# A plan of rounds for every batch: projection pieces, value runs and the mixer's steps placed anew

## The chip, the core and the metric

The kernel runs on one NeuronCore of a Trainium2 chip. The metric is the device time of one execution in microseconds (us). The kernel before was timed three times: 812.35 us is the median, 811.07 and 813.69 us are the ends.

A NeuronCore has five engines that take their instructions in order, each from its own queue: TensorE (PE, matrix products and transposes), VectorE (DVE), ScalarE (ACT), GpSimd (POOL), and SyncE (SP), which issues most DMAs. They wait for one another through semaphores.

## The reference

Three blocks follow each other, on 4 batches of 768 tokens with 512 channels.

```python
# 1. chunked local attention, 8 heads of 64: chunks of 32 queries see 16 keys to the left, 8 to the right, 8 memory keys
a = softmax(scale * q_c @ concat(mem_k, k_ctx).T);  out[chunk] = a @ concat(mem_v, v_ctx)
# 2. four experts of causal attention (width 64), each token keeps its best two
logits = x @ w_gate                       # top 2 of 4, softmax over them
for e in range(4):
    q, k, v = x @ wq[e], x @ wk[e], x @ wv[e]
    ye = softmax(causal(scale * q @ k.T)) @ v @ wo[e]
    out += gate[e] * ye
# 3. mixer: a rank-32 product along the sequence, then a two-layer network of 2048 hidden channels
u = x + (x.T @ U @ V).T
out = u + relu(u @ w_ch1) @ w_ch2
```

## The kernel before

The first part of the program, up to some 415 us of the span, does blocks 1 and 2 and the sequence mixing of block 3; the rest does the two-layer network. Only the first part is touched here.

Each batch goes through 12 *rounds*. A round belongs to a pair of experts and a tile of 128 query tokens: `ROUNDS` lists tiles 0 to 2 of pair 0, tiles 0 to 2 of pair 1, then tiles 3 to 5 of both. The function `rnd` writes the instructions of one round:

- a *unit* of local attention (two heads, half the sequence, of the next batch, or of batch 0 in the first rounds): scores `s` (L534), softmax in `a`, transposes `tp` (L562) that are copied to `at`;
- the round's expert scores `sc` (L673 and L675), softmax in `ac` (DVE L694, ACT L696, POOL L731);
- the transposes `tpc` (L751) of the round before, copied to `ath` (L754) by ACT and DVE in turn;
- up to three *pieces* of work taken from a list: a projection of queries and keys (`pqk`, L593) or of values (`pv`, L633);
- in some rounds a *run*: the products that use only a part of the array's columns, one after the other, into `t` and `t2` (L829): local values (`t<-at`), expert values (`t<-ath`), and the mixer's first product (`t<-y`).

The run is written with a higher priority, and its first product waits for all copies that any product of the run reads (`READY` in `rnd`); the products behind it follow in order.

Which round has a run is said by `SESSIONS`, how many pieces a round takes by `FILL` (batch 0: `FILL0`), which round starts a unit by `S_AT`. A run takes the expert values of rounds that were transposed before the last one; for a pair (batch, round) in `FRESH` it takes the last one's too.

The mixer has, for each pair of a batch, four steps: `mix_turn` transposes the result `yT` (`pyt`, L779) and copies it to `y`; `mix_down` multiplies `y` with U as a part of a run; `mix_keep` makes `qm` of it on ACT and DVE; `mix_up` multiplies `qm` with V (`pz`, L809), adds and stores it. Their rounds stand in the loop as numbers that hold for all batches: turn of pair 1 in round 2 of the next batch, its down in round 3, its up in round 7 (last batch: 4); turn of pair 0 in round 10, its down in round 11, its up in round 0 of the next batch.

In the last batch, pieces of the network's first product (`ph`, L366; `po`, L383) and of the product of weights (`w1p`, L313) fill the rounds.

The Tile framework's scheduler then orders each engine's instructions, so rounds overlap in the built program. PSUM tiles rotate between two buffers: `sc`, `tpc`, `pyt` and the wide `pz` share one pair, `s` and `tp` another. A tile's first write waits until the readers of the tile two before it are done.

Of the kernel before, what the change touches and what calls it, by code (L numbers as in the profile page):

```python
# [29 lines left out]
NT = S // 128  # L30
# [8 lines left out]
NIDLE = 4  # L39
WLOAD = {1: ((0,), ()), 2: ((1,), ()), 3: ((2, 3), ()), 5: ((), (0, 1))}  # L40
WSPLIT = {2: ((0,), ()), 3: ((1, 2), ()), 4: ((3,), ()), 5: ((), (0, 1))}
FILL = (1, 1, 2, 1, 1, 1, 1, 1, 1, 1, 1, 2)
S_AT0 = (2, 3, 4, 5, 6, 7, 9, 10)
FILL0 = (0, 0, 0, 3, 2, 2, 0, 1, 2, 1, 2, 1)
S_AT = (0, 1, 3, 4, 5, 6, 8, 9)
NAC = 7
AHEAD = 400
NLIN = 2
# [3 lines left out]
NLT = 5  # L52
NLA = 1
NAT = 8
SESSIONS = {0: (0, 2, 4, 6, 8, 9, 11), 1: (1, 3, 5, 7, 9, 11), 2: (1, 3, 5, 7, 9, 11), 3: (1, 3, 5, 7, 9, 11)}
FRESH = ((0, 9), (1, 9), (2, 9), (3, 9), (3, 11))
NXP = 8
FS = 1
HG = 1
# [45 lines left out]
def tile_chunk_attention__moe_attention__mixer(  # L105
# [309 lines left out]
    with ExitStack() as p1:  # L415
# [349 lines left out]
        def keep(b, pr, i, pav):  # L765
            if i == 0:
                pool, kw_ = (cw, dict(bufs=2)) if b % 2 or (b, pr) == (B - 2, 1) else (dp0, dict(tag=f"wp_{'hl'[pr]}0", bufs=1))
                yT[b, pr] = pool.tile([128, S], F32, name="yT", **kw_)
            nc.scalar.copy(yT[b, pr][:, i * 128:(i + 1) * 128], pav)

        ys, qms, ys_ins = {}, {}, {}

        def mix_turn(b, pr):
            y = ys[b, pr] = cw.tile([128, NT, 128], F32, name="y", tag="ac", bufs=NAC)
            p = ps.tile([128, 1024], F32, name="pyt", **TC)
            for t in range(NT):
                tr = nc.tensor.transpose(p[:, t * 128:(t + 1) * 128], yT[b, pr][:, t * 128:(t + 1) * 128], ident_s)  # L779
            hold['p4'] = tr.ins  # L780
            ys_ins[b, pr] = [nc.scalar.copy(y[:, :4], p[:, :512].rearrange("p (t f) -> p t f", f=128)).ins,
                             nc.vector.tensor_copy(y[:, 4:], p[:, 512:768].rearrange("p (t f) -> p t f", f=128)).ins]
# [50 lines left out]
        def rnd(new=None, old=None, s_unit=None, o_unit=None, fill1=(), fill2=(), down=None, then=None, late=(), locs=()):  # L833
            if s_unit:
                local_load(s_unit)
                if then:
                    load_weights(*then)
                local_scores(s_unit, 0)
            turned = []

            def between():
                if o_unit:
                    local_turn(o_unit, 0)
                turned.append(1)
            if new:
                scores(*new, between)
            if not turned:
                between()
            if s_unit:
                local_scores(s_unit, 1)  # L850
            if o_unit:
                local_turn(o_unit, 1)
            for f in fill1:
                f()
            if old:
                turn_scores(*old)
            for f in fill2:
                f()
            if not (locs or late or down):
                return  # L860
            free = [ps.tile([128, 512], F32, name="t", **TE)]
            if len(locs) == 2 or locs and len(late) + bool(down) > 1:
                free.append(ps.tile([128, 512], F32, name="t2", **TQ))
            pos = [x[:, :HALF] for x in free[:len(locs)]]
            places = [x[:, o:o + 128] for n, x in enumerate(free) for o in ((HALF,) if n < len(locs) else (HALF, 256, 128, 0))]
            with tc.high_priority(AHEAD):
                session.clear()
                behind = [x for v in late for x in turned_ins.pop(v)] + [x for u in locs for x in half[u]["ins"]]
                if down:
                    behind += ys_ins.pop(down[:2])  # L870
                kept = [(v, places.pop(0)) for v in late]
                for n in range(max(len(locs), 1)):
                    if locs:
                        local_values(locs[n], pos[n])
                    for v, p in kept[n:n + 1] if n + 1 < len(locs) else kept[n:]:
                        values(*v, p)
                if down:
                    pq = places.pop(0)
                    mix_down(*down, pq)
                for x in behind:  # L880
                    tc.add_manual_dep(session[0], x.name, READY, reason="start of a run on parts of the array")
                for x, y in zip(session, session[1:]):
                    tc.add_manual_dep(y, x.name, QUEUE, reason="run on parts of the array")
            for v, p in kept:
                keep(*v, p)
            for u, p in zip(locs, pos, strict=True):
                local_split(u, p)
            if down:
                mix_keep(*down, pq)
# [38 lines left out]
        def batch_half(b, hf):  # L928
            return [(b, hp, hf) for hp in range(HP)]
# [3 lines left out]
        for _ in range(NWARM):  # L933
            p = ps.tile([128, 512], F32, name="pwarm", **TL)
# [19 lines left out]
                nc.vector.memset(row_s[:, :S - 128], 0.0)  # L954
                nc.vector.tensor_copy(row_s[:, S - 128:], tri_s)
        load_mixer()
        old, mixed, turned, locs = None, {}, [], []
        for b in range(B):
            last = b == B - 1
            s_at = {} if last else dict(zip(S_AT0 if b == 0 else S_AT, batch_half(b + 1, 0) + batch_half(b + 1, 1)))  # L960
            before = None
            if b == 0:
                s_at.update(zip(range(8), units[PRO:]))
                before = units[PRO - 1]
            work = pieces(b, 1) + ([] if last else pieces(b + 1, 0))
            for r, (pr, i) in enumerate(ROUNDS):
                n = (FILL0 if b == 0 else FILL)[r] if work else 0
                ending[0] = last and r >= 10
                f1, f2, work = work[:n][:1], work[:n][1:], work[n:]
                if b and r == 2:  # L970
                    f2 = f2 + [lambda: mix_turn(b - 1, 1)]
                if b and r == (4 if last else 7):
                    f1 = [lambda: mix_up(b - 1, 1)] + f1
                if r == 10:
                    f2 = f2 + [lambda: mix_turn(b, 0)]
                if b and r == 0 and not mixed.get(b - 1):
                    f1 = [lambda: mix_up(b - 1, 0)] + f1
                down = (b, 0) if r == 11 else (b - 1, 1) if b and r == 3 else None
                o_unit = s_at.get(r - 1) if r else before
                locs += [o_unit] if o_unit else []  # L980
                now, wait = turned, [old] if old else []
# [2 lines left out]
                if r in SESSIONS[b]:  # L984
                    rnd((b, pr, i), old, s_at.get(r), o_unit, f1, f2, down, late=now, locs=locs)
                    turned, locs = wait, []
                else:
                    rnd((b, pr, i), old, s_at.get(r), o_unit, f1, f2)
                    turned = turned + [old] if old else turned
                old = (b, pr, i)  # L990
# [35 lines left out]
    with ExitStack() as p2:  # L1026
# [45 lines left out]
        late = list(range(NEC, NCH))  # L1072
# [80 lines left out]
        for k, (c, f) in enumerate(steps):  # L1153
# [36 lines left out]
            if store and not todo:  # L1190
                (c_, pt_), = store
                store = []
                if not nx:
                    with tc.issue_after(ended[0]):
                        pr = [residual(c_, m, TLAST[m]) for m in range(KT)]
                else:
                    pr = None
# [79 lines left out]
```

## Time and profile before

| | |
|---|---|
| median of three runs | 812.35 us (811.07 to 813.69) |
| the profiled execution | 814.0 us, of which the span from the first to the last instruction is 811.9 us |
| PE busy | 784.9 us, 97% of the span |
| DVE, ACT, POOL busy | 620.5, 497.2, 159.4 us |
| share of the chain that ended last | PE 70%, DVE 16%, ACT 6%, DMA 5% |

A row of the timeline names the start, the time that the row's instructions took together, the engine, the source line, the operation, what it writes and reads, and how often. In brackets stands how long the engine sat idle before the row, and whose instruction released it. A matmul's recorded time is longer than its step to the next one, since matmuls overlap. Products of fp32 operands (`s`, `t`) have two records each.

### The profile page before, as it was taken

What the parts mean: (1) busy time and instruction counts of PE and PEld (TensorE: products, weight loads), DVE (VectorE), ACT (ScalarE), POOL (GpSimd) and SP (SyncE); (2) the same over time, 40 slices, a digit from 0 to 9 for tenths busy, and PEclk for the clock granted to TensorE, in tenths of its full rate; (3) what the DMA queues carried; (4) which work ended last, traced back from release to release, by engine and by line L of the source; (5) the groups of instructions that cost most, each with busy time, mean ns of one, the idle gap of its engine ahead of it and who ended that gap; (6) DMA issues with size and microseconds to landing.
All of it is one profiled execution on the core that took longest, in us unless ns stands there. A gap on an engine that the chain in (4) does not pass through costs nothing.

```text
span 811.9 us, 17863 instructions
## 1 busy us (share of the span) xinstructions
PE 784.9 (97%) x6382; PEld 710.2 (87%) x6382; DVE 620.5 (76%) x2029; ACT 497.2 (61%) x1448; POOL 159.4 (20%) x244
## 2 busy tenths in 40 slices
PE   7989999999999999998999999999999999999997
PEld 5779998989999897887888888999999999999996
DVE  6687878687778769996468799989587595875956
ACT  6787767677668756665445567665455564555642
POOL 4554434444343513313000000000000000000000
PEclk9999999999999999999999999999999999999999
DMA  9443353333333105153037635103003030030211
GB/s 287 123 149 95 92 144 110 93 91 111 92 96 100 43 9 219 53 175 130 15 115 236 199 101 181 53 1 131 1 4 128 1 114 16 2 131 1 78 53 52
DMA packets 36792, 77.67 MB, mean 96 GB/s; under 512 B 4192, under 2 KB 12896, under 8 KB 35936
## 3 DMA queue, kind: packets, MB, share of 16 engines
q1 hardware_dynamic: 36416, 76.21, 29.1%
q8 instruction: 50, 0.82, 0.4%
q14 instruction: 38, 0.31, 0.1%
q10 hardware_dynamic: 288, 0.32, 0.1%
HBM read 60.79 MB, written 15.73 MB: 94 GB/s over the span
## 4 chain that ended last, share of the span: by engine, by line
PE 70%; DVE 16%; ACT 6%; DMA 5%; issue 3%; POOL 0%; DVEq 0%; ACTq 0%; POOLq 0%; SPq 0%
PE acc L1150 25%; PE ph L366 14%; PE t L829 6%; PE pqk L593 5%; PE pv L633 3%; PE s L534 3%; PE po L383 3%; PE tpc L751 3%; DMA raw<-in_w 2%; PE sc L673 2%; PE sc L675 2%; PE tp L562 2%; ACT a L541 2%; DVE d_t L144 1%; DMA part<-o 1%
## 5 line engine op out<-in xcount | busy, mean ns | idle before, releaser
L1150 PE MATMUL acc<-xhi,sw 128*128 128x256 f32 x1008 | 187.9, 282 | 0.1
L1150 PEld LDWEIGHTS acc<-xhi,sw 128*128 128x128 f32 x1008 | 159.3, 189 | 4.8 <-ACT xhi L1068 0.3
L1150 PE MATMUL acc<-xlo,sw 128*128 128x256 f32 x504 | 139.1, 282 | 0.2 <-DVE xlo L1069 0.2
L1065 DVE TENSOR_TENSOR sx<-t 128x256 f32<-128x256 f32 x180 | 67.9, 423 | 66.8 <-ACT t L1058 66.7
L1058 ACT ACTIVATE t<-ph 128x512 f32<-128x512 f32 x72 | 43.0, 598 | 99.4 <-PE ph L366 99.3
L1150 PEld LDWEIGHTS acc<-xlo,sw 128*128 128x128 f32 x504 | 95.5, 190 | 2.4 <-DVE xlo L1069 0.4
L731 POOL TENSOR_SCALAR ac<-ac,su,g 128x128 f32<-128x128 f32 (+5 forms) x92 | 69.0, 758 | 104.8 <-DVE su L729 27.5
L1068 ACT CAST xhi<-sx 128x256 fp32r<-128x256 f32 x205 | 74.8, 406 | 22.0 <-DVE sx L1065 19.0
L541 ACT ACTIVATE a<-a,nm 128x96 f32<-128x96 f32 x192 | 69.9, 366 | 20.1 <-DVE nm L538 19.7
L1069 DVE TENSOR_TENSOR xlo<-sx,xhi 128x256 fp32r<-128x256 f32 x205 | 77.0, 424 | 3.0 <-ACT xhi L1068 2.2
L366 PE MATMUL ph<-zh,wp_l 128*128 128x512 f32 x192 | 61.4, 398 | 0.3 <-DVE hl L376 0.3
L366 PE MATMUL ph<-zh,wp_h 128*128 128x512 f32 x192 | 60.9, 394 | 0.0
L751 PE MATMUL tpc<-ident_s,ac 128*128 128x128 f32 x336 | 53.1, 277 | 6.3 <-POOL ac L731 2.6
L696 ACT ACTIVATE ac<-ac,nmc 128x128 f32<-128x128 f32 (+5 forms) x72 | 47.8, 665 | 17.9 <-DVE nmc L694 17.3
L546 POOL TENSOR_TENSOR a<-a,rs 128x288 f32<-128x288 f32 x64 | 43.2, 678 | 77.3 <-DVE rs L545 35.8
L534 PE MATMUL s<-k_t,q_t 128*128 128x96 f32 (+1 forms) x480 | 52.3, 269 | 5.1 <-DMA k_t<-in_kw 1.5
L366 PE MATMUL ph<-zl,wp_h 128*128 128x512 f32 x176 | 55.6, 394 | 0.0
L534 PEld LDWEIGHTS s<-k_t,q_t 128*128 128x128 f32 (+1 forms) x480 | 46.5, 172 | 10.0 <-issue 5.3
L694 DVE CUSTOM_DVE_ANT_0 ac<-sc,row_s 128x128 f32<-128x128 f32 (+5 forms) x72 | 43.3, 618 | 11.0 <-PE sc L675 10.5
L538 DVE CUSTOM_DVE_ANT_0 a<-s,band_s 128x96 f32<-128x96 f32 x192 | 39.8, 250 | 14.5 <-PE s L534 13.8
L751 PEld LDWEIGHTS tpc<-ident_s,ac 128*128 128x128 f32 x336 | 38.5, 141 | 13.6 <-POOL ac L731 5.8
L673 PE MATMUL sc<-kl,qs 128*128 128x384 f32 (+2 forms) x144 | 48.2, 340 | 1.3 <-DVE ath L754 0.6
(209 smaller groups left out, 1952.5 us busy)
## 6 DMA issues: line engine op xcount, KB each, us to landing
raw<-in_w SPq DMA_DIRECT2D x42, 256.0 KB, 3.6
v_t<-in_vw SPq DMA_DIRECT2D x32, 288.0 KB, 4.1
q_t<-in_qT SPq DMA_DIRECT2D x24, 384.0 KB, 3.2
k_t<-in_kw SPq DMA_DIRECT2D x31, 220.0 KB, 3.5
part<-o SPq DMA_DIRECT2D x24, 256.0 KB, 2.9
pt<-part SPq DMA_DIRECT2D x6, 1024.0 KB, 4.8
out<-pt SPq DMA_DIRECT2D x24, 256.0 KB, 2.3
raw<-in_w SPq DMA_DIRECT2D x11, 512.0 KB, 3.8
```

The costliest lines, as they stand in the source:

```text
L366: nc.tensor.matmul(p, w[f // 4][:, pr, fs], z[:, pr], start=(n == 0), stop=(n == 5))
L534: last = nc.tensor.matmul(s[own, j, :], w["q"][own, qd * 3 + j], k_g[own], start=True, stop=True).ins
L541: nc.scalar.activation(a[:, j, :], a[:, j, :], AF.Exp, bias=nm[:, j:j + 1], scale=-1.0, accum_out=ss[:, j:j + 1])
L673: nc.tensor.matmul(s[:, o:o + w], q, kl[b, e, hf][:, :w], start=True, stop=False)
L696: nc.scalar.activation(a, a, AF.Exp, bias=nm[:, h:h + 1], scale=-1.0, accum_out=su[:, h:h + 1])
L731: (nc.vector if ending[0] else nc.gpsimd).tensor_scalar(aa[h][:, :n], aa[h][:, :n], su[:, h:h + 1], gates[b, i // 3][:, i % 3, 2 * pr + h: ...
L751: hold['t', 6 * (i // 3) + 3 * pr + i % 3] = nc.tensor.transpose(tp[h][:, j * 128:(j + 1) * 128], aa[h][:, j * 128:(j + 1) * 128], ident_s ...
L829: session.append(nc.tensor.matmul(*a, **kw).ins)
L1065: nc.vector.tensor_tensor(x, t[:, p[0], p[1]], t[:, q[0], q[1]], op=op)
L1068: nc.scalar.copy(hi, x)
L1069: nc.vector.tensor_sub(lo, x, f32(hi))
L1150: ended[0] = nc.tensor.matmul(acc[n][:, m], w[:, ms], x, start=(f == FA and u == 0 and m == 0), stop=(f == NF - 2 and u == 2 and m == 1)).ins
```

## The change

The tables get one entry per batch, and the rounds of the mixer's steps become tables too. `SESSIONS` has other rounds in batches 0, 1 and 3; `FRESH` has 12 pairs where it had 5. Nothing is computed differently: each engine has the same instructions with the same operands' shapes, in another order. The rename from `kept` to `keeps` makes room for a counter that is checked while the program is built.

```diff
-FILL = (1, 1, 2, 1, 1, 1, 1, 1, 1, 1, 1, 2)
...
-FILL0 = (0, 0, 0, 3, 2, 2, 0, 1, 2, 1, 2, 1)
...
+FILL = ((0, 0, 0, 3, 1, 2, 0, 2, 0, 3, 1, 2),
+        (1, 1, 3, 1, 1, 0, 0, 2, 1, 1, 1, 2),
...
-SESSIONS = {0: (0, 2, 4, 6, 8, 9, 11), 1: (1, 3, 5, 7, 9, 11), 2: (1, 3, 5, 7, 9, 11), 3: (1, 3, 5, 7, 9, 11)}
-FRESH = ((0, 9), (1, 9), (2, 9), (3, 9), (3, 11))
+SESSIONS = {0: (1, 2, 4, 5, 6, 7, 9, 10, 11), 1: (0, 1, 3, 4, 5, 7, 9, 11), 2: (1, 3, 5, 7, 9, 11), 3: (1, 3, 5, 10, 11)}
+FRESH = ((0, 0), (0, 9), (0, 10), (0, 11), (1, 3), (1, 9), (2, 9), (3, 3), (3, 5), (3, 7), (3, 9), (3, 11),)
+TURN1, DOWN1, UP1 = (5, 2, 2, 2), (2, 4, 3, 3), (3, 9, 9, 5)
+TURN0, DOWN0, UP0 = (10, 10, 10, 11), (11, 11, 11, 11), (4, 2, 3, 0)
...
-                n = (FILL0 if b == 0 else FILL)[r] if work else 0
+                n = FILL[b][r]
...
-                if b and r == 2:
+                if b and r == TURN1[b]:
                     f2 = f2 + [lambda: mix_turn(b - 1, 1)]
-                if b and r == (4 if last else 7):
+                if b and r == UP1[b]:
                     f1 = [lambda: mix_up(b - 1, 1)] + f1
-                if r == 10:
+                if r == TURN0[b]:
                     f2 = f2 + [lambda: mix_turn(b, 0)]
-                if b and r == 0 and not mixed.get(b - 1):
+                if b and r == UP0[b]:
                     f1 = [lambda: mix_up(b - 1, 0)] + f1
-                down = (b, 0) if r == 11 else (b - 1, 1) if b and r == 3 else None
+                down = (b, 0) if r == DOWN0[b] else (b - 1, 1) if b and r == DOWN1[b] else None
```

In the built order the network part behind 415 us is the same on PE. In the first part PE has 44 runs of part-array products before, and 40 now. Three places follow; the line numbers of the kernel now are 3 to 6 higher.

PE from the end of batch 0 into batch 1, before: the run that ends with the mixer's first product, and what follows up to `pz`.

```order
L829 MATMUL t_2228<-at,v_t 64x64 x12
L829 MATMUL t_2228<-y,u_s 32x128 x6
...
L751 MATMUL tpc<-ident_s,ac 128x128 x12
L534 MATMUL s<-k_t,q_t 128x96 x3
L562 MATMUL tp<-ident_s,a 96x128 x3
L673 MATMUL sc<-kl,qs 128x256
L675 MATMUL sc<-kd,qs 128x256
L673 MATMUL sc<-kl,qs 128x256
L675 MATMUL sc<-kd,qs 128x256
L751 MATMUL tpc<-ident_s,ac 128x128
L809 MATMUL pz<-v_st,qm 128x384 x2
```

The same place now.

```order
L835 MATMUL t_2254<-y,u_s 32x128 x6
L565 MATMUL tp<-ident_s,a 96x128 x3
L596 MATMUL pqk<-xl,wqk_h 128x384 x4
L596 MATMUL pqk<-xh,wqk_h 128x384 x4
L596 MATMUL pqk<-xh,wqk_l 128x384 x4
...
L596 MATMUL pqk<-xl,wqk_h 128x384 x4
L596 MATMUL pqk<-xh,wqk_h 128x384 x4
L596 MATMUL pqk<-xh,wqk_l 128x384 x4
...
L835 MATMUL t<-at,v_t 64x64 x12
L835 MATMUL t<-ath,vt 64x128 x12
...
L815 MATMUL pz<-v_st,qm 128x384
```

Two projection pieces and a run, which stood behind `pz`, now stand between the mixer's first product and `pz`.

PE in round 3 of batch 3, before: the run that ends with the mixer's first product for the pair 1 of batch 2.

```order
L633 MATMUL pv<-wvg_l,xh 128x260
L673 MATMUL sc<-kl,qs 128x128
L675 MATMUL sc<-kd,qs 128x128
L673 MATMUL sc<-kl,qs 128x128
L675 MATMUL sc<-kd,qs 128x128
...
L829 MATMUL t<-ath,vt 64x128 x6
L829 MATMUL t<-y,u_s 32x128 x6
L751 MATMUL tpc<-ident_s,ac 128x128 x3
L366 MATMUL ph<-zh,wp_l_5496 128x512 x2
```

The same run now.

```order
L754 MATMUL tpc<-ident_s,ac 128x128 x3
L369 MATMUL ph<-zh,wp_l_5503 128x512 x2
...
L754 MATMUL tpc<-ident_s,ac 128x128 x3
L676 MATMUL sc<-kl,qs 128x256
L678 MATMUL sc<-kd,qs 128x256
L676 MATMUL sc<-kl,qs 128x256
L678 MATMUL sc<-kd,qs 128x256
...
L835 MATMUL t<-ath,vt 64x128 x12
L835 MATMUL t<-y,u_s 32x128 x6
```

The run stands 12 `ph` products and a round of scores later, and now reads the copies of the transposes `tpc` that stand just ahead of it.

PE in round 8 of batch 3, before: the scores of the second expert of the pair, and the transposes of round 7.

```order
L383 MATMUL po<-hh,w2h_5595 128x512
L673 MATMUL sc<-kl,qs 128x384
L675 MATMUL sc<-kd,qs 128x384
L673 MATMUL sc<-kl,qs 128x384
L675 MATMUL sc<-kd,qs 128x384
...
L751 MATMUL tpc<-ident_s,ac 128x128 x10
```

The same scores now.

```order
L676 MATMUL sc<-kl,qs 128x384
L678 MATMUL sc<-kd,qs 128x384
L676 MATMUL sc<-kl,qs 128x384
L678 MATMUL sc<-kd,qs 128x384
...
L386 MATMUL po<-hl,w2h_5620 128x512
L386 MATMUL po<-hh,w2h_5620 128x512
...
L386 MATMUL po<-hl,w2h_5620 128x512
L386 MATMUL po<-hh,w2h_5620 128x512
L754 MATMUL tpc<-ident_s,ac 128x128 x10
```

14 `po` products, which stood ahead of these scores, now stand between them and the transposes.

## Rows read from the trace of the kernel before

**Rows 1.** The page: busy us, share of the span, instructions of each engine.

```profile
PE 784.9 (97%) x6382; PEld 710.2 (87%) x6382; DVE 620.5 (76%) x2029; ACT 497.2 (61%) x1448; POOL 159.4 (20%) x244
```

**Rows 2.** Windows: stretch, its length, busy us of each engine, PEclk, DMA.

```profile
45.00:57.00 12.00, 9.80 (x105) 8.02 (x102) 10.94 (x69) 10.88 (x47) 8.41 (x16) 1.00 0.34 105
57.00:130.00 73.00, 73.00 (x782) 69.93 (x780) 55.26 (x245) 53.30 (x185) 31.34 (x50) 1.00 0.39 114
130.00:138.00 8.00, 6.55 (x52) 5.24 (x49) 7.21 (x35) 5.34 (x25) 3.00 (x5) 1.00 0.54 176
138.00:165.00 27.00, 27.00 (x274) 25.76 (x273) 19.12 (x101) 18.60 (x72) 11.25 (x17) 1.00 0.28 84
165.00:170.00 5.00, 3.20 (x26) 2.69 (x24) 4.84 (x23) 3.42 (x12) 2.23 (x4) 1.00 0.41 124
170.00:174.00 4.00, 4.00 (x45) 3.50 (x43) 2.58 (x13) 2.88 (x12) 3.65 (x7) 0.57 0.30 78
174.00:220.00 46.00, 45.83 (x489) 43.53 (x488) 34.27 (x140) 32.24 (x104) 17.41 (x26) 1.00 0.32 96
220.00:226.00 6.00, 4.88 (x44) 3.89 (x43) 5.77 (x22) 4.69 (x18) 3.41 (x5) 1.00 0.35 103
226.00:300.00 74.00, 73.07 (x752) 68.72 (x753) 54.28 (x240) 49.75 (x173) 29.04 (x47) 1.00 0.21 66
300.00:376.00 76.00, 72.35 (x512) 61.38 (x511) 69.18 (x148) 50.32 (x121) 23.60 (x30) 1.00 0.41 144
376.00:415.00 39.00, 35.70 (x299) 29.36 (x298) 19.57 (x38) 16.49 (x37) 3.47 (x4) 1.00 0.13 50
415.00:811.90 396.90, 390.65 (x2586) 357.57 (x2585) 307.39 (x804) 219.19 (x528) 0.00 (x0) 1.00 0.23 80
```

**Rows 3.** Timeline of PE: local scores without and with a run behind them.

```profile
84.34 0.80 PE L534 MATMUL s<-k_t,q_t 128*128 128x96 f32 x6
84.98 0.49 PE L562 MATMUL tp<-ident_s,a 128*96 128x128 f32 x3
...
86.44 0.91 PE L534 MATMUL s<-k_t,q_t 128*128 128x96 f32 x6
87.28 0.92 PE L829 MATMUL t<-at,v_t 96*64 96x64 f32 x24
88.03 0.39 PE L829 MATMUL t<-ath,vt 128*64 128x128 f32 x4
88.35 0.42 PE L562 MATMUL tp<-ident_s,a 128*96 128x128 f32 x2
```

**Rows 4.** Timeline of PE: waits in batch 1.

```profile
167.63 0.41 PE L751 MATMUL tpc<-ident_s,ac 128*128 128x128 f32 x2 [1.06 <-DVE nmc L694]
168.79 0.91 PE L534 MATMUL s<-k_t,q_t 128*128 128x96 f32 x6 [0.74 <-DVE nm L538]
```

**Rows 5.** Timeline of DVE: weight rows decoded among batch 1's work.

```profile
158.82 0.76 DVE L293 CAST wt_h<-d_r 128x512 fp32r<-128x512 f32 x2
...
164.72 0.76 DVE L145 SCALAR_TENSOR_TENSOR d_t<-raw,d_t 128x256 uint32<-128x256 uint32 x2
```

**Rows 6.** Timeline of PE: the mixer's first product and `pz`, batch 0 to 1.

```profile
129.46 0.85 PE L829 MATMUL t<-y,u_s 128*32 128x128 f32 x12
...
136.36 0.62 PE L809 MATMUL pz<-v_st,qm 96*128 96x384 f32 x2 [0.43 <-DVE qm L799]
```

**Rows 7.** Timeline of PE: waits in batch 3.

```profile
330.64 0.88 PE L829 MATMUL t<-ath,vt 128*64 128x128 f32 x12 [0.89 <-DVE y L782]
...
382.46 1.84 PE L751 MATMUL tpc<-ident_s,ac 128*128 128x128 f32 x12 [1.16 <-POOL ac L731]
...
385.36 2.84 PE L829 MATMUL t<-ath,vt 128*64 128x128 f32 x48 [0.19 <-DVE ath L754]
```

**Rows 8.** Windows, `po` products (L383) alone: length, PE's and weight loads' busy us, clock.

```profile
373.70:376.40 2.70, 2.70 (x13) 2.06 (x11) 1.00 1.01 330
```

**Rows 9.** Groups of instructions: ACT's copies of transposed scores (busy us, mean ns).

```profile
L754 ACT COPY ath<-tpc 128x384 f32<-128x384 f32 (+5 forms) x52 | 27.0, 519 | 8.5 <-PE tpc L751 8.1
```

More of the change, by code (lines that the diff above doesn't have):

```diff
@@ L41 @@
 WSPLIT = {2: ((0,), ()), 3: ((1, 2), ()), 4: ((3,), ()), 5: ((), (0, 1))}
-FILL = (1, 1, 2, 1, 1, 1, 1, 1, 1, 1, 1, 2)
-S_AT0 = (2, 3, 4, 5, 6, 7, 9, 10)
-FILL0 = (0, 0, 0, 3, 2, 2, 0, 1, 2, 1, 2, 1)
-S_AT = (0, 1, 3, 4, 5, 6, 8, 9)
+FILL = ((0, 0, 0, 3, 1, 2, 0, 2, 0, 3, 1, 2),
[3 rows of a table added]
+S_AT = ((2, 3, 4, 5, 6, 7, 9, 10), (0, 1, 3, 4, 5, 6, 8, 9), (0, 1, 3, 4, 5, 6, 8, 9))
 NAC = 7
@@ L769, in keep @@
             nc.scalar.copy(yT[b, pr][:, i * 128:(i + 1) * 128], pav)
+            kept[b, pr] = kept.get((b, pr), 0) + 1
         ys, qms, ys_ins = {}, {}, {}
+        kept = {}
         def mix_turn(b, pr):
+            assert kept[b, pr] == NT
             y = ys[b, pr] = cw.tile([128, NT, 128], F32, name="y", tag="ac", bufs=NAC)
@@ L870, in rnd @@
                     behind += ys_ins.pop(down[:2])
-                kept = [(v, places.pop(0)) for v in late]
+                keeps = [(v, places.pop(0)) for v in late]
                 for n in range(max(len(locs), 1)):
@@ L874, in rnd @@
                         local_values(locs[n], pos[n])
-                    for v, p in kept[n:n + 1] if n + 1 < len(locs) else kept[n:]:
+                    for v, p in keeps[n:n + 1] if n + 1 < len(locs) else keeps[n:]:
                         values(*v, p)
@@ L883, in rnd @@
                     tc.add_manual_dep(y, x.name, QUEUE, reason="run on parts of the array")
-            for v, p in kept:
+            for v, p in keeps:
                 keep(*v, p)
@@ L956, in tile_chunk_attention__moe_attention__mixer @@
         load_mixer()
-        old, mixed, turned, locs = None, {}, [], []
+        old, turned, locs = None, [], []
         for b in range(B):
             last = b == B - 1
-            s_at = {} if last else dict(zip(S_AT0 if b == 0 else S_AT, batch_half(b + 1, 0) + batch_half(b + 1, 1)))
+            s_at = {} if last else dict(zip(S_AT[b], batch_half(b + 1, 0) + batch_half(b + 1, 1)))
             before = None
```

2 rows, old and new, of the table FILL are left out of this document.

## The prediction

> **What bounds the kernel now.** I read the page first: PE is busy for 784.9 of 811.9 us [rows 1]. So PE is the bound, and as the change gives it the same instructions, it can win or lose only two things on PE: idle time, and steps in which the array is busy but slower than it could be. The windows come next [rows 2]. Up to 57 us and from 130 us on they show where PE idles; behind 415 us the order on PE does not change, so its 396.9 us stay. Idle time is a stretch's length less PE's busy time: 2.20 us in 45 to 57, 1.45 in 130 to 138, 1.80 in 165 to 170, 0.17 in 174 to 220, 1.12 in 220 to 226, 0.93 in 226 to 300, together 7.7 us in batches 0 to 2. The last batch has 3.65 in 300 to 376 and 3.30 in 376 to 415, together 6.9 us [rows 2]. The stretch 57 to 130, and 138 to 165, have none. One more loss shows in the clock column: 170 to 174 ran at 0.57 of the full clock, which is the lower of the two levels (1.2 instead of 2.4 GHz) for most of it, right behind the stretch with 1.80 us of idle time in 5 [rows 2]. 4 us at 0.57 are 1.7 us lost. The timelines then say what PE waited for in these places, and those are the rows on which the parts below rest. Before 45 us the order is nearly the same in both kernels, so nothing is counted there.
>
> **The change part by part.** The profiled execution took 814.0 us, 2.1 us of them outside the span. The sum is made against it and then set beside the median.
>
> *Fewer runs.* There are 44 runs of part-array products before and 40 now. What a run costs beyond its products: six local scores are followed by the next instruction 0.64 us later where that is a transpose (84.34 to 84.98), and 0.84 us later where it is a run (86.44 to 87.28): 0.20 us at the way in. At the way out, the last four products take 0.32 us to the next instruction (88.03 to 88.35) [rows 3], where four of the long run take 4 x 0.054 = 0.22 us (2.84 us less the last one's 0.27, over 47 steps) [rows 7]: 0.10 us. 4 x 0.30 = **1.2 us** less. Its bounds are 0.8 us (0.20 each, if the way out hides) and 1.2 us.
>
> *The mixer's up at the start of batches 1 and 2.* In batch 1, `pz` waited 0.43 us for `qm`, though the products that `qm` is made of had ended 6 us before (129.46 + 0.85 = 130.3): VectorE, 7.21 of 8 us busy there, came to it late [rows 2, 6]. Now 24 projection products and a run stand between. The transposes and scores around it get their work later too, since `pz` and the first projection changed places with them. Of 1.45 us I take 1.3 as gone. In batch 2, 220 to 226, `pz` moves from round 0 to 3, and the transposes of the last round have more work ahead of them: 0.9 of 1.12 us.
>
> *The stretch 165 to 170.* PE waited 1.06 us for a transpose's softmax and 0.74 us for local scores' buffers, both released by VectorE's maxima [rows 4]. VectorE was 4.84 of 5 us busy [rows 2]. What fills it there beyond a round's usual work are weight rows for batch 3 (two casts at 158.82, the decoding that ends at 164.72 + 0.76 = 165.5) on top of the expert gates of half a batch and the mixer's `qm` [rows 5]. In the order now the weight rows still fall into batch 1, behind the same unit's values, but the gates lie ahead of them and `qm` behind. I take 1.4 of 1.80 us as gone. Below 300 us there remain 0.93 us in 226 to 300, of which I take 0.6: ahead of the scores that waited there (at the end of batch 2) now stand a value piece and more transposes. At 45 to 57 all three, VectorE 10.94, ScalarE 10.88 and GpSimd 8.41 of 12 us, are near full [rows 2]; moving work inside this stretch shifts the wait more than it ends it, and I take 0.3 of 2.20. Together 1.3 + 0.9 + 1.4 + 0.6 + 0.3 = **4.5 us**. The bounds are 0 (VectorE's load is the same, and each wait reappears at the next reader) and 7.7 us (all of it).
>
> *The last batch.* The run at 330.64 waited 0.89 us for the mixer's `y` [rows 7]; it now stands 12 `ph` products later, so this goes. The transposes at 382.46 waited 1.16 us for GpSimd [rows 7]; they, and the two groups ahead of them, now have 14 `po` products between the scores and themselves. 13 of them touch a stretch of 2.70 us, so one takes 0.21 us or a little more and 14 take 3 us [rows 8]; that is more than the 1.16 us waited. The first 7 us of batch 3 keep their order and their waits. Of 6.9 us I take **2.6 us** as gone; bounds 0.9 (the one wait whose cause is moved away entirely) and 4.0 us. The mixer's turn of pair 0 goes from round 10 to 11 here, and its copy `y` is now read by a run with only six transposes between: that gives back what the scores behind the old place gain, and I count it as zero.
>
> *New waits of runs.* By `FRESH` more runs now start close behind the transposes whose copies they read. I count seven in the new order with less than about 2 us of PE work between (batch 0: four; batch 1: one; batch 2: one; batch 3: one), and three of this kind that vanish. No such wait is in the trace for those seven, so bounds: the run at 385.36 stood as close and waited 0.19 us; the run at 330.64 waited 0.89 us, the longest [rows 7]. 7 x 0.19 = 1.3 and 7 x 0.89 = 6.2 us. Two copies on ScalarE after one another are 2 x 0.519 us [rows 9], and the closest runs leave 0.3 to 0.6 us of work to hide them; so most of the seven are nearer to the low row: 0.33 each, **2.3 us** more. Behind a waiting run stands all of PE, since its queue is in order.
>
> *Thinner cover elsewhere.* Some softmax chains get less PE work between scores and transposes (round 3 of batch 2 has half of what it had). The longest wait of this kind in the trace is 1.06 us [rows 4]; two of them at a low share make **0.8 us** more, bounds 0 and 2.1.
>
> *DMA.* The store of `z` goes out two to four rounds later and local loads swap places on SP's queue; up to 415 us PE's waits of any length that the rows show are on engines, none on a transfer, so I take 0; a round late it would cost one wait of the size of 0.74 us.
>
> The sum: -1.2 - 4.5 - 2.6 + 2.3 + 0.8 = -5.2 us, and -1.7 us for the clock if its fall goes with the idle time before it. 814.0 - 6.9 = 807.1 us. The profiled execution lies 1.65 us above the median, about what the fall cost, so I take the median to be without it: 812.35 - 5.2 = 807.15 us. Both ways lead to **807.2 us**.
>
> **The clock.** In the trace the clock fell once in batches 0 to 2, behind 1.80 us of idle time in 5 us, and it did not fall at 45 to 57 with 2.20 us in 12, nor at 130 to 138 with 1.45 in 8 [rows 2]. The Trainium skill, "TensorE: Matmul & The Clock Gate", section "A second HAM failure mode: psum-queue depth-cycling", says that short idle spells between groups of matmuls, when frequent, make the clock go to and fro between its levels. By that rule the runs that wait for fresh copies would be such spells; the trace agrees with it in one place and not in the two others. What it would do here is the second rival below.
>
> **The rivals.**
>
> 1. *VectorE is the bound, and waits only move.* It is 69.2 of 76 us busy in 300 to 376, and 10.94 of 12 at the start of batch 0 [rows 2], and its instructions are the same. Then only the runs (1.2 us), the two waits for `qm` and the ones at 330.64 and 382.46 go (0.4 + 0.4 + 0.9 + 1.2, less the 2.3 + 0.8 us of new ones): about -1 us, 811.3 us. Against it: between 57 and 300 us its share is 0.76, so there is room to move in. Chance 0.2.
>
> 2. *The clock falls in a new place.* Runs that wait for fresh copies, together with a scores' wait close by, idle as much as 165 to 170 did, and 1.7 us are lost again: 807.2 + 1.7 = 808.9 us. For it: the fall in batch 1. Against it: the runs are spread over three batches. Chance 0.15.
>
> 3. *Runs wait for their copies.* The mechanism for slower: every run that reads fresh copies stands still until the slower of two engines has come to them, in places where VectorE is late by more than a microsecond. The other terms together win 1.2 + 4.5 + 2.6 - 0.8 = 7.5 us, so it decides from (7.5 + 2.4) / 7 = 1.4 us a run, more than any row shows (0.89); at 1.6 us a run the time is 812.35 - 7.5 + 11.2 = 816 us. Chance 0.08.
>
> 4. *Every wait at stake goes.* With 7.0 us in batches 0 to 2, 4.0 in batch 3, 1.2 for the runs and 1.3 for new waits: -10.9 us, 801.5 us. Chance 0.1.
>
> That the change does not do what it says is excluded: the order shows the moves.
>
> **How the numbers follow.** My forecast has 0.47, the rivals 0.2, 0.15, 0.08 and 0.1. Leaving out half of the best case and the slow one, the range is 803 to 812 us; its upper end holds rival 1. A measurement of this kernel can tell about 0.3%, 2.4 us, from no change: faster is below 809.9 us. The forecast, rivals 2 and 4 lie there, and a little of each may miss it: 0.69 for faster; rival 1 and what misses make 0.23 for the same; 0.08 for slower.
>
> **What would show it.** In the new profile: 40 runs; no wait of `pz` for `qm` in batches 1 and 2; in batch 1 no five microseconds with more than 1 us of idle PE, and a clock of 1.00 throughout; PE's idle time from 45 to the end of batch 3's part down from 14.6 to about 9.5 us. The part behind it keeps its 396.9 us to within 0.3. I am wrong if the runs in rounds 0 to 2 of batch 0 and round 3 of batch 3 wait for `ath` or `at` by more than 0.7 us each, or if the idle time in 300 to 415 us does not fall.

## The result and the profile after

The kernel after takes 804.5 us (median of four runs, 803.59 to 805.38); the kernel before took 813.0 us (median of four, 811.07 to 815.46). The ratio is 0.9894 (0.9863 to 0.9924): 8.5 us less, where 5.2 were forecast.

The page of the kernel after, PE's row of part 1, answers to [rows 1]. The profiled execution took 803.96 us, its span 801.9.

```profile
PE 780.4 (97%) x6382; PEld 708.4 (88%) x6382; DVE 620.4 (77%) x2029; ACT 496.9 (62%) x1448; POOL 158.9 (20%) x244
```

PE is busy 4.5 us less with the same instructions, and 5.5 us less idle (801.9 - 780.4 = 21.5, before 811.9 - 784.9 = 27.0). To see where, I cut both executions where PE stands at the same work: the first scores of batch 1, those of the last round of batch 2, the mixer's last product of batch 3, and the first `acc` of the network. The columns are those of [rows 2]. Before:

```profile
130.32:298.70 168.38, 163.20 (x1653) 152.52 (x1654) 126.88 (x564) 115.68 (x409) 69.54 (x108) 0.99 0.28 86
298.70:412.10 113.40, 106.16 (x794) 89.07 (x793) 88.38 (x184) 66.22 (x157) 27.19 (x34) 1.00 0.32 113
412.10:498.17 86.07, 85.07 (x448) 71.93 (x447) 72.73 (x201) 52.31 (x128) 0.00 (x0) 1.00 0.52 173
```

The same stretches of the kernel after:

```profile
128.79:289.93 161.14, 159.41 (x1675) 150.43 (x1673) 128.36 (x559) 115.44 (x404) 71.63 (x111) 1.00 0.29 87
289.93:402.62 112.69, 106.23 (x793) 89.03 (x792) 87.42 (x184) 65.40 (x156) 25.53 (x34) 1.00 0.33 114
402.62:488.23 85.61, 84.77 (x448) 72.04 (x448) 72.79 (x201) 52.37 (x128) 0.00 (x0) 1.00 0.52 174
```

Batches 1 and 2 are 7.24 us shorter, batch 3 is 0.71 us shorter, and the stretch behind it, whose order on PE is the same, 0.46 us. (The first stretch is not quite the same work: by the records of the trace, batch 0 now does ten local scores and six transposes more, and 36 part-array products fewer; at some 0.11, 0.11 and 0.05 us from one to the next, that nearly cancels.) The first stretch also begins 1.5 us earlier, 0.9 us of which was there at the first value products (13.60 us, before 14.48), behind waits for loads. So some 1.4 us (0.9 and the 0.46) of the 10.05 us between the two profiled executions are most likely no effect of the change.

In batches 1 and 2 PE's idle time fell from 5.18 to 1.73 us (length less busy time). The places of the prediction: at the start of batch 1, which had [rows 6], the timeline of PE after shows no idle time.

```profile
133.09 0.85 PE L835 MATMUL t<-y,u_s 128*32 128x128 f32 x12
133.87 0.53 PE L565 MATMUL tp<-ident_s,a 128*96 128x128 f32 x3
134.16 0.94 PE L596 MATMUL pqk<-xl,wqk_h 128*128 128x384 f32 x4
134.94 0.86 PE L596 MATMUL pqk<-xh,wqk_h 128*128 128x384 f32 x4
...
145.32 0.43 PE L815 MATMUL pz<-v_st,qm 96*128 96x384 f32 x1
```

`pz` comes 11 us behind the mixer's product instead of 6, and what stood behind it fills the time. The waits of [rows 4], 1.06 and 0.74 us, became two others in the same round, 1.05 and 0.20 us. VectorE's rows show what the longer one waits for, the copy `at` right behind the decoding of the weight rows:

```profile
169.80 0.50 PE L565 MATMUL tp<-ident_s,a 128*96 128x128 f32 x3 [1.05 <-DVE at L567]
170.50 0.55 PE L754 MATMUL tpc<-ident_s,ac 128*128 128x128 f32 x3 [0.20 <-DVE ath L757]
...
167.66 1.53 DVE L148 SCALAR_TENSOR_TENSOR d_t<-raw,d_t 128x256 uint32<-128x256 uint32 x2
169.11 0.54 DVE L567 COPY at<-tp 96x384 f32<-96x384 f32 x1
```

The last step of that decoding took 0.76 us before [rows 5] and 1.53 us here, for the same two instructions. GpSimd was idle during it before (161.97 to 165.76 us) and works beside it here; whether that is the cause was not tested.

In batch 3 the wait of [rows 7] at 330.64 is gone from its instruction: the run that now holds the mixer's product starts without a bracket, but a wait of 1.06 us stands 4.5 us ahead of it. The other wait, at 382.46, is not gone. The same twelve transposes, at 373.01 now, wait 1.08 us where they waited 1.16, for another engine (timelines of PE, POOL and ACT, after):

```profile
322.01 1.10 PE L369 MATMUL ph<-zh,wp_l 128*128 128x512 f32 x2 [1.06 <-DVE wp_l L338]
...
326.50 1.53 PE L835 MATMUL t<-ath,vt 128*64 128x128 f32 x24
327.97 0.85 PE L835 MATMUL t<-y,u_s 128*32 128x128 f32 x12
...
368.89 1.95 POOL L734 TENSOR_SCALAR ac<-ac,su,g 128x768 f32<-128x768 f32 x2 [0.57 <-ACT ac L702]
...
372.08 0.69 ACT L702 ACTIVATE ac<-sc,nmc 128x512 f32<-128x512 f32 x1 [1.75 <-DVE nmc L727]
...
373.01 1.52 PE L754 MATMUL tpc<-ident_s,ac 128*128 128x128 f32 x12 [1.08 <-ACT ac L702]
```

The softmax that they read is done at 370.84 (368.89 + 1.95), 2.2 us before they start. That leaves their PSUM tile. It shares its pair of buffers with the scores `sc` of the next round, which stand right ahead of them and are read by ScalarE up to 372.8.

And of the runs that read fresh copies in batches 0 to 2, the longest wait is this one, 0.24 us:

```profile
55.19 0.92 PE L835 MATMUL t<-at,v_t 96*64 96x64 f32 x24 [0.24 <-DVE ath L757]
```

### The profile page after: what moved, and what is told of

Same layout as the page of the kernel before. It is cut to its first block, busy times and chain, and to the rows that moved or that the text cites. A ratio compares the mean times of both kernels' runs of the same rounds, so it can differ in the third digit from the quotient of the medians.

```text
span 801.9 us, 17854 instructions
## 1 busy us (share of the span) xinstructions
PE 780.4 (97%) x6382; PEld 708.4 (88%) x6382; DVE 620.4 (77%) x2029; ACT 496.9 (62%) x1448; POOL 158.9 (20%) x244
## 4 chain that ended last, share of the span: by engine, by line
PE 73%; DVE 14%; DMA 5%; ACT 4%; issue 3%; DVEq 0%; ACTq 0%; SPq 0%
PE acc L1156 25%; PE ph L369 14%; PE t L835 7%; PE pqk L596 6%; PE pv L636 4%; DMA raw<-in_w 4%; PE tpc L754 4%; PE s L537 3%; PE po L386 2%; PE sc L676 2%; PE tp L565 2%; PE sc L678 2%; DVE d_t L147 1%; DVE d_t L148 1%; DVE a L541 1%
## 5 line engine op out<-in xcount | busy, mean ns | idle before, releaser
L537 PE MATMUL s<-k_t,q_t 128*128 128x96 f32 (+1 forms) x480 | 50.6, 268 | 2.4 <-DMA k_t<-in_kw 1.7
```

What stands on the lines that cost most here:

```text
L537: last = nc.tensor.matmul(s[own, j, :], w["q"][own, qd * 3 + j], k_g[own], start=True, stop=True).ins
```

## The experiments

Each kernel ran beside the kernel before; its median and ratio are given. "On before" and "on after" say which of the two the edit is made on.

### One batch's new plan at a time

On before: the new entries of `FILL`, `SESSIONS`, `FRESH` and the mixer's tables for one batch, the old ones for the others. For batch 2, for instance, that is (written with the new tables)

```diff
-        (1, 1, 2, 1, 1, 1, 1, 1, 1, 1, 1, 2),
+        (2, 0, 2, 0, 2, 1, 1, 1, 1, 1, 1, 2),
-UP1 = (3, 7, 7, 4);  UP0 = (4, 0, 0, 0)
+UP1 = (3, 7, 9, 4);  UP0 = (4, 0, 3, 0)
```

> Batch 0 alone has its new plan, batches 1 to 3 the old one. Theory A (the gain lies in batches 0 to 2, each plan works by itself): at points of equal TensorE work the new trace gained 0.6 us between the first scores of batch 0 and of batch 1, so -0.6 us (-1.5 to 0.3). Rival B (the plans work only together, since runs carry values over from batch to batch): 0 or slower.

> Batch 1 alone has its new plan. Theory A: 3.6 us were gained between the first scores of batch 1 and of batch 2, 1.7 of them the clock; so -3.6 us (-4.5 to -1.5, the smaller end if the executions of the kernel before mostly have no fall of the clock there), and the waits of 0.43 us for qm and of 1.06 and 0.74 us for VectorE's maxima are smaller. Rival B: under 1 us.

> Batch 2 alone has its new plan. Theory A: 3.3 us were gained up to round 10 of batch 2, so -3.3 us (-4 to -2); the waits at its start (1.1 us in all) and at the scores of round 9 (0.62 us) are gone. Rival B: under 1 us.

> Batch 3 alone has its new plan. Theory A (VectorE and ScalarE bound this part, so waits only move): -0.5 us (-1.2 to 0.5), TensorE's idle time in the last batch within 0.8 us of 6.9. Rival C (the plan of batch 3 gives the 2.6 us of the prediction, and loses them elsewhere in the full change): -2.6 us.

| new plan in | median (us) | ratio | less than 812.97 |
|---|---|---|---|
| batch 0 | 808.40 | 0.9940 (0.9923 to 0.9957) | 4.6 |
| batch 1 | 809.22 | 0.9952 (0.9934 to 0.9970) | 3.8 |
| batch 2 | 808.91 | 0.9949 (0.9930 to 0.9968) | 4.1 |
| batch 3 | 812.77 | 0.9995 (0.9983 to 1.0008) | 0.2 |

Batch 3's plan gives nothing that can be measured; the 2.6 us forecast for it are not there. The other three give 12.4 us one by one, more than the 8.5 of all four. For batches 1 and 2 that is theory A's size (3.6 and 3.3 us expected); batch 0 was expected to give 0.6 us, 1.5 at most, and I had missed what its plan does. It changes what is left for batch 1, so the wait at the start of batch 1 goes with it too; in its trace the `pz` of [rows 6], still in round 0, has no wait in front:

```profile
135.93 0.60 PE L815 MATMUL pz<-v_st,qm 96*128 96x384 f32 x2
```

So the gains overlap where two plans take away the same waits. At the start of batch 1 (1.29 us in three brackets before) no bracket in front of `pz` or the transposes is left with batch 0's plan alone, nor with batch 1's alone. At the start of batch 2 (0.99 us before) 0.44 us are left with batch 0's plan and none with batch 2's, but batch 1's alone makes it 2.07 us. PE's idle time in batches 1 and 2 falls by 1.79, 1.73 and 1.76 us with the plans of batches 0, 1 and 2 alone, 5.28 together; with all three it falls by 3.86 (next section).

The kernel with batch 3's new plan alone has the order of before in batches 1 and 2 and had no fall of the clock there:

```profile
131.85:299.21 167.36, 161.70 (x1653) 151.13 (x1654) 127.15 (x564) 115.58 (x409) 69.71 (x108) 1.00 0.28 86
```

Against before's 163.20 us PE is busy 1.50 us less: that is about what the fall behind 170 us [rows 2] cost in the profiled execution.

### Batches 0 to 2 together

On after: the old entries for batch 3.

> The kernel after with the old plan in batch 3, so the new plans of batches 0 to 2 together. Theory A (in batch 3 the new plan only moves the waits): within 0.7 us of the kernel after, so about 804.5 to 805. Rival B (the prediction's 2.6 us from batch 3 are there, and were hidden in the single run of that plan): 807. Besides, its sum tells how far the single plans of batches 0, 1 and 2 (-4.6, -3.8, -4.1 us) overlap: 12.5 us if they don't, about 8 if they remove the same waits.

804.24 us, ratio 0.9885 (0.9865 to 0.9905): the kernel after has 0.9894, so A. The three plans overlap by 12.4 - 9.1 = 3.3 us, hardly more than the four intervals leave open together (some 3 us); the idle times above overlap by 1.4 us. The windows of this kernel in batches 1 and 2, in batch 3, and in a part of batch 3:

```profile
131.21:292.03 160.82, 159.50 (x1675) 150.50 (x1673) 127.93 (x559) 115.38 (x404) 71.60 (x111) 1.00 0.29 87
292.03:404.37 112.34, 106.83 (x793) 90.29 (x793) 87.37 (x184) 66.04 (x156) 27.46 (x34) 0.98 0.33 114
...
300.00:310.00 10.00, 8.81 (x46) 8.25 (x47) 9.54 (x18) 6.57 (x17) 2.07 (x4) 0.83 0.71 273
```

With the old plan batch 3 is no longer than with the new one (112.34 to 112.69 us), even with 10 us at 0.83 of the clock, which is 1.7 us lost.

### The mixer's up alone

On before: `pz` of pair 0 moves to a round two later in batch 1 and three later in batch 2. Four products change places, and with them the additions to `z` and its stores.

```diff
-UP0 = (4, 0, 0, 0)
+UP0 = (4, 2, 3, 0)
```

> The kernel before, with one edit alone: the mixer's up of pair 0 moves from round 0 to round 2 in batch 1 and from round 0 to round 3 in batch 2. Theory A (the idle time at the start of a batch is pz that stands ahead of VectorE's qm, and what is behind it): the 1.45 us of idle in 130 to 138 and the 0.99 us at 222 to 226 go, so about 2 us less than before, 811. Rival B (VectorE is late there, and the next transposes and scores wait in its place): within 0.5 us of before. If A holds, the new plans of batches 0, 1 and 2 each contain this gain or a part of it, which is why their single gains add up to more than the whole.

807.93 us, ratio 0.9930 (0.9907 to 0.9952): 5.4 us less (3.9 to 7.6), more than A's 2, and 0.64 of what the whole change gives. Windows of batches 1 and 2, and of 7 us in them:

```profile
129.36:294.11 164.75, 161.98 (x1654) 152.78 (x1655) 125.34 (x564) 115.22 (x409) 69.79 (x108) 0.99 0.29 87
...
165.00:172.00 7.00, 5.80 (x69) 4.99 (x69) 5.20 (x26) 4.75 (x21) 4.29 (x8) 0.76 0.44 131
```

The two batches are 3.63 us shorter; the rest of the 5.4 us lies outside them, where PE has the same work, and is not explained. Idle time is 2.77 us instead of 5.18, which is A's 2.4. But PE is also busy 1.22 us less, with a fall of the clock as large as before's (7 us at 0.76 are 1.7 us, as were 4 at 0.57). One place shows where that comes from. At the start of batch 2, before had these two waits:

```profile
222.38 0.84 PE L751 MATMUL tpc<-ident_s,ac 128*128 128x128 f32 x6 [0.16 <-DVE ath L754]
224.05 0.85 PE L751 MATMUL tpc<-ident_s,ac 128*128 128x128 f32 x6 [0.83 <-DVE rs L545]
225.03 0.62 PE L809 MATMUL pz<-v_st,qm 96*128 96x384 f32 x2
```

With `pz` moved, the projections that had stood behind it come forward, between the two groups of transposes (the timeline of this kernel):

```profile
220.07 0.87 PE L754 MATMUL tpc<-ident_s,ac 128*128 128x128 f32 x6
220.70 0.96 PE L596 MATMUL pqk<-xl,wqk_h 128*128 128x384 f32 x4
221.49 0.86 PE L596 MATMUL pqk<-xh,wqk_h 128*128 128x384 f32 x4
222.20 0.86 PE L596 MATMUL pqk<-xh,wqk_l 128*128 128x384 f32 x4
222.90 0.81 PE L754 MATMUL tpc<-ident_s,ac 128*128 128x128 f32 x6
```

From the first group of transposes to the second PE needed 1.67 us before (222.38 to 224.05), for work that takes 0.63 (220.07 to 220.70): 1.04 us lost, of which 0.83 are written as idle. Here a wait cost some 0.2 us more than its bracket says, since the last product ahead of it counts as busy until its modelled end, where a product without a wait behind it overlaps with the next. By the same reading, a wait shorter than that need not show as idle at all. So fewer waits also lower the busy time. That all of the 1.22 us are of this kind is an inference from this place: before has eight brackets in the two batches and this kernel five, and three at 0.2 us are half of it.

### The weight rows on VectorE later

On before: the rows of [rows 5] come behind unit 21 instead of unit 17.

```diff
-                        behind_x.append(17)
+                        behind_x.append(21)
```

> The kernel before, with one edit alone: the weight rows that VectorE casts and decodes from 158 to 165 us (for batch 3) come behind the work of unit 21 instead of unit 17, some ten microseconds later. Theory A (these rows make VectorE late, the transposes and local scores at 167 to 169 wait for its maxima, 1.8 us, and the clock falls behind that): 1.8 us less than before, and 3.5 where the clock would have fallen there. Rival B (VectorE has the same work in the batch, and the wait moves to where the rows go): within 0.5 us of before.

811.50 us, ratio 0.9971 (0.9956 to 0.9986): 1.9 us less, A's size without the clock. The waits of [rows 4] are 0.21 us now, and one of 0.92 us came up at 198 us (the timeline of this kernel):

```profile
166.65 0.91 PE L534 MATMUL s<-k_t,q_t 128*128 128x96 f32 x6 [0.21 <-DVE nm L538]
...
198.34 0.92 PE L829 MATMUL t<-at,v_t 96*64 96x64 f32 x24 [0.92 <-DVE ath L754]
```

So the prediction's reason for the stretch 165 to 170 holds. But PE's idle time in batches 1 and 2 fell by 0.70 us only in this execution (5.18 to 4.48): a part of the wait moved on, as rival B said. The new plan leaves these rows behind unit 17, and there the wait is 1.05 us in the profiled execution of after, and 0.67 us in that of the kernel with the old plan in batch 3, whose order is the same here.

### The mixer's up back, in the kernel after

On after: `UP0` goes back to round 0 in batches 1 and 2.

```diff
-UP0 = (4, 2, 3, 0)
+UP0 = (4, 0, 0, 0)
```

> The kernel after, with one part undone: the mixer's up of pair 0 goes back to round 0 in batches 1 and 2. Alone on the kernel before that part gave 5.4 us. Theory A (the other moves of the new plan don't reach these waits): 3.5 to 5.4 us over after, about 809. Rival B (the other moves give the same places more work in front, as the plan of batch 0 alone already did at 130 to 138): 0 to 1.5 us over after, 804.5 to 806. The trace should have waits of pz for qm at the start of batches 1 and 2 under A and none above 0.2 us under B.

807.25 us, ratio 0.9927 (0.9913 to 0.9941): 2.7 us over after, between A and B. The longest wait of `pz` for `qm` in batches 1 and 2 is 0.21 us, as B said. The stretch of both batches, and the longest wait in it:

```profile
129.35:293.45 164.10, 160.78 (x1675) 150.73 (x1673) 127.52 (x559) 115.29 (x404) 71.50 (x111) 1.00 0.29 86
```

```profile
169.35 0.27 PE L565 MATMUL tp<-ident_s,a 128*96 128x128 f32 x1
170.88 0.50 PE L565 MATMUL tp<-ident_s,a 128*96 128x128 f32 x3 [1.26 <-POOL kl L624]
```

It is 2.96 us longer than after's 161.14, 1.59 idle and 1.37 busy, in waits of 0.15 to 0.26 us (one of 0.42) besides this one, spread over both batches. So the other moves cover the wait for `qm` itself, but not what `pz` in round 0 takes from the rounds behind it. Which of these short waits hangs on it is not settled.

### The same move in batch 3, and what should have been better still

On after: `UP0` gets a 2 for batch 3. Then, on the kernel with the plans of batches 0 to 2 alone, that move and the later weight rows together.

```diff
-UP0 = (4, 2, 3, 0)
+UP0 = (4, 2, 3, 2)
```

> The kernel after, with one edit alone: in batch 3 too the mixer's up of pair 0 moves from round 0 to round 2. It is the one place left where pz waits for qm (0.67 us at 299.71, behind 0.69 us for the transposes at 298.17). Theory A (pz ahead of a late qm is what costs, wherever it stands): 1.0 to 1.5 us under after, about 803.3. Rival B (from 300 us on VectorE has no gap, so what is gained is lost at its next reader, as the rest of batch 3's plan was): the same as after. Rival C (the store of z leaves later and the next stage's load of it comes late): over after by 0.5 us or more.

> What the runs so far point to: the new plans of batches 0 to 2, the old one in batch 3 (0.35 us shorter there by the trace), the mixer's up of pair 0 in batch 3 at round 2 instead of 0, and the weight rows on VectorE behind unit 21 instead of 17. If each takes its wait away (0.35, 1.3 and the 1.05 us that are left at 169.80): 2 to 2.7 us under after, about 802. If VectorE in batch 3 and the other order in batch 1 have taken these places over: the same as after within 0.7 us.

805.28 us, ratio 0.9904 (0.9889 to 0.9920), and 807.65 us, ratio 0.9928 (0.9916 to 0.9941). The first is within the noise of after, the second 2.8 us over it by the ratios. Batch 3 takes 114.29 and 115.63 us in them (112.69 after, and 112.34 in the kernel on which the second is made), at a clock of 1.00 (the row is the first kernel's). So the move that pays in batches 1 and 2 gains nothing here. The later rows did take away the wait of 1.05 us in batch 1, yet batches 1 and 2 take 160.87 us with them and 160.82 without; what part they have in the longer batch 3 is not separated from the move's.

```profile
289.50:403.79 114.29, 106.77 (x793) 89.08 (x793) 86.20 (x184) 65.61 (x156) 26.54 (x34) 1.00 0.32 112
```

The two waits at 298 and 300 are gone in the first, and three others follow within 10 us (its timeline):

```profile
306.21 2.62 PE L835 MATMUL t<-ath,vt 128*64 128x128 f32 x44 [0.86 <-DVE ath L757]
...
314.39 0.41 PE L754 MATMUL tpc<-ident_s,ac 128*128 128x128 f32 x2 [0.68 <-DVE ath L757]
315.43 0.76 PE L785 MATMUL pyt<-ident_s,yT 128*128 128x128 f32 x5 [0.63 <-ACT ac L702]
```

No version that I ran beats the kernel after by more than its uncertainty.

### Work off VectorE in batch 3

On after: `load_w2` passes GpSimd to the subtraction in `decode_row`.

```diff
-        decode_row(w2[f], w2h[f], w2l[f], raw2.pop(f), nc.vector)
+        decode_row(w2[f], w2h[f], w2l[f], raw2.pop(f), nc.gpsimd)
```

> The kernel after, with one edit alone: the subtraction that makes the low part of the second weight's rows (four instructions, 0.67 us each) is on GpSimd instead of VectorE. Theory A (in batch 3 VectorE has no gap from 300 to 330 us, and that is why the wait at 330.64 came back at 322.01 as a wait for VectorE's wp_l, 1.06 us): the wait at 322 goes and the whole is 1.0 to 1.5 us under the kernel after, about 803. Rival B (the wait only moves on once more): the same as after, 804.5. Rival C (GpSimd is slower at it and the low parts come late): 1 us or more over after.

809.03 us, ratio 0.9945 (0.9928 to 0.9963): 4.1 us over after by the ratios, rival C and more (in its profiled execution 10 us of batch 3 ran at 0.83 of the clock, 1.7 us of this). The line's instructions, with min, median and max in ns:

```profile
L176 DVE TENSOR_TENSOR w_l<-d_t,w_h x4: 679/682/686, 295.8 to 315.7; 128x512 fp32r<-128x512 f32 x4
L176 POOL TENSOR_TENSOR w2l<-d_t,w2h x4: 1292/1513/1762, 319.1 to 329.1; 128x512 fp32r<-128x512 f32 x4
```

The wait for `wp_l` is still there with 0.79 us. And VectorE, which I had taken for the bound, stood idle behind the slower step (its timeline):

```profile
321.60 0.80 DVE L146 TENSOR_SCALAR d_t<-d_t 128x512 uint32<-128x512 uint32 x1 [1.23 <-ACT d_t L145]
```

The decoding of a row is a chain through two buffers in turn: ScalarE scales, VectorE shifts, ScalarE makes the high part, and the subtraction frees the buffer for the row after the next. A step of 1.51 us for 0.68 makes the chain longer. In the kernel after VectorE has hardly a gap there (4.97 of 5 us busy at 318 to 323), but taking work from it did not help; that PE waits for the length of the chain is what these rows suggest.

### More runs

On after: late value products may run in all 12 rounds of batches 1 and 2.

```diff
-SESSIONS = {..., 1: (0, 1, 3, 4, 5, 7, 9, 11), 2: (1, 3, 5, 7, 9, 11), ...}
+SESSIONS = {..., 1: (0, 1, 2, 3, 4, 5, 6, 7, 8, 9, 10, 11), 2: (0, 1, 2, 3, 4, 5, 6, 7, 8, 9, 10, 11), ...}
```

> The kernel after, with one edit alone: in batches 1 and 2 the late value products may run in every round, which cuts the same products into five more runs (44 for 39 in the order). Theory A (a run costs 0.30 us at its two ends, read from the trace of before): 1.5 us over after. Rival B (the ends lie beside other work): 0. Rival C (each new run also waits for its copies, by the 0.33 us that the prediction took for a fresh run): 3 us over.

804.76 us, ratio 0.9893 (0.9880 to 0.9907): the same as after, which is B; the two intervals are too wide to exclude A's 1.5 us by the time alone. The windows:

```profile
129.26:288.90 159.64, 159.19 (x1687) 149.77 (x1685) 126.41 (x556) 116.33 (x403) 70.95 (x111) 1.00 0.29 88
288.90:404.04 115.14, 108.49 (x782) 91.91 (x781) 88.31 (x187) 66.43 (x156) 26.44 (x34) 0.99 0.33 112
...
288.90:320.00 31.10, 28.61 (x218) 25.58 (x218) 27.61 (x58) 20.13 (x47) 11.99 (x16) 0.95 0.42 149
```

PE is busy 267.68 us over both (after 265.64). Of the 2.04 us more, 31.1 us at 0.95 of the clock are 1.55; some 0.5 are left for five runs, 0.1 each. Idle time is 7.10 us (after 8.19). So by the trace a run's ends cost less than 0.30 us here, and less idle time makes up for it; that this is because a run that is cut lies in more places as work to wait behind was not shown.

## Why the prediction was right, step by step

*Direction and place: right.* The gain lies mostly in batches 1 and 2 (7.24 us between the profiled executions): idle time that other work in front of the waits took away, and busy time that went with it. PE's idle time from 45 us to the end of batch 3 fell from 14.62 to 10.09 us, where about 9.5 were forecast. That this comes so close is partly luck: two terms below failed, -2.6 and +2.3 us, and they cancel.

*Waits in batches 0 to 2 (4.5 us forecast): right in cause, too small in size.* At 130 to 138 all 1.45 us went (1.3 forecast). At 220 to 226 the waits of 0.16 and 0.83 us went too (0.9 forecast); `pz` itself had no bracket there. At 278.86 0.62 us went (0.6). In 165 to 170 0.55 us went instead of 1.4: the weight rows, whose part in it is shown by their move, stayed behind the same unit. So the sign "no five microseconds of batch 1 with more than 1 us of idle PE" did not come. Over batches 1 and 2 idle time fell by 3.45 us. Besides, PE's busy time fell by 3.79, of which about 1.5 were the clock. The rest, 2.3 us, is explained in part at best: I had priced waits by their brackets alone; with `pz` alone moved, the busy time fell by 1.22 us beside 2.41 us of idle time, so the brackets may leave out up to a third.

*The start of batch 1 hangs on more than one table.* I gave its gain to the move of `pz`. Batch 0's plan alone removes it as well, and it alone gives 4.6 us, where I counted 0.3 us for batch 0's rounds. In those rounds 0.3 was about right: from 15 us to the cut PE idles 4.06 us (before 4.20).

*Fewer runs (-1.2 us): the count was right, 40, the price too high by the trace.* Five runs more cost about 0.1 us of busy time each, not 0.30, and moved the time by nothing measurable.

*The last batch (-2.6 us): failed.* Its plan alone gives 0.2 us, and without it the kernel is as fast. The step that failed is that work put between a softmax's scores and its transposes ends the wait at the transposes. At 382.46 the 14 `po` products did what I said for the softmax, but the scores of the next round stand right ahead of these transposes in both kernels, and the PSUM tile was the second condition. The last reader of that tile is ScalarE's first exponential of those scores, in before:

```profile
381.28 0.69 ACT L699 ACTIVATE ac<-sc,nmc 128x512 f32<-128x512 f32 x1 [1.73 <-DVE su L729]
```

With its read of the sum it ends at 382.05 there. In the kernel after the transposes start 0.15 us behind that end; so in before this condition alone would have held them to some 382.2 (an estimate), where they started at 382.46. I had looked at the last releaser alone. Besides, 0.87 us went at 378.79, but a wait of 0.93 us for the same step of ScalarE is new at 353.73, 15 us behind the end of the softmax that is read there (338.4). And the 0.89 us at 330.64 went, but 1.06 for `wp_l` came. Idle time in batch 3 fell by 0.78 us (7.24 to 6.46). That waits only move is what rival 1 said, and it holds in batch 3 alone; the move of `pz` gains nothing there.

*New waits of runs (+2.3 us): failed, to the good side.* Of the seven runs one shows a wait, 0.24 us at 55.19; the others start without a bracket. The copies were done in the 0.3 to 0.6 us of work in front, which I had thought too little, and rival 3 falls.

*Thinner cover (+0.8 us): not seen.* In batches 1 and 2 no bracket above 0.2 us stands before transposes that read an expert softmax, and the 1.08 and 0.93 us in batch 3 are for PSUM tiles.

*The clock (-1.7 us in the profiled execution alone): right there, wrong for the median.* I took the median of before to be free of falls. Of the 44 runs of before beside the experiments, 18 had a mean granted clock of at least 0.999 (median 812.0 us) and 26 a lower one (median 814.0). Of the 75 runs of the twelve changed kernels, 30 had at least 0.999, a like share. So falls come and go in one and the same order, and cost about 2 us where they come. Without falls the change gives about as much: 812.0 us before, and 804.0 in the three of after's four runs that had at least 0.999. The kernel before fell to 0.57 behind the waits of [rows 4]; the one with batch 3's new plan alone had the same two waits (1.05 and 0.74 us), as much idle time, and 4 us at 1.00 behind them (windows, the 5 us with the waits and the stretch behind):

```profile
166.70:171.70 5.00, 3.21 (x25) 2.53 (x24) 4.84 (x24) 3.58 (x13) 2.32 (x5) 1.00 0.43 124
...
171.70:175.70 4.00, 4.00 (x67) 3.73 (x68) 3.72 (x16) 3.17 (x12) 3.73 (x7) 1.00 0.30 80
```

The rule that the prediction took from the Trainium skill ("TensorE: Matmul & The Clock Gate", section "A second HAM failure mode: psum-queue depth-cycling") agrees with one of these two executions and not with the other. Over all profiled executions it holds in one direction: between 20 us and the last microseconds the clock fell eight times, each time right behind 5 us in which PE idled for 1.6 to 2.1 us, but not behind every such place. Rival 2's place, the runs that wait for fresh copies, shows no fall; three of the kernels made from after fell at the start of batch 3, behind waits of the transposes and `pz`.

## What to carry to other kernels

When an engine that takes its work in order has a small step with a long chain behind it, look first at where that step stands: moving four products gave nearly two thirds of what a whole new plan gave. Price a wait by the distance between the starts around it, not by the idle time alone. Before a wait is taken for gone, look for the second condition behind the one that the profile names: the same twelve transposes waited 1.16 us for a softmax and then 1.08 us for their PSUM tile. Test the parts of a plan both alone and left out; parts that remove the same waits look like separate gains.

## What was not expected of the hardware

The same subtraction of 128x512 elements took 0.68 us on VectorE and 1.51 us on GpSimd.

The granted clock falls to its lower level for a few microseconds at places that differ between executions. PE can be busy throughout such a stretch, but in no trace was it ahead of it: in the kernel with batch 0's plan alone PE idled 2.11 of the 5 us before, and then the clock was 0.51 (windows).

```profile
371.40:376.40 5.00, 2.89 (x20) 2.31 (x19) 2.92 (x6) 2.76 (x6) 1.36 (x2) 1.00 0.16 61
376.40:379.90 3.50, 3.50 (x19) 3.17 (x18) 1.37 (x4) 1.19 (x3) 2.11 (x3) 0.51 0.01 2
```
